# Products of the second MLP matrix on one pair of TensorE tiles, and its last chunk in four transfers

## The chip, the cores and the metric

The kernel runs on one core of a Trainium2 chip. The metric is the device time of one execution in microseconds (us); times are medians of several executions, all in the fast state where a state can be told. Profiles give the span on the core, about 1.3 us shorter than that time. In their lines PE is TensorE (PEld its weight loads), DVE is VectorE, ACT ScalarE, POOL GpSimd and SP SyncE, which issues the transfers.

## The reference, cut to what matters

A decode step for eight tokens mixes a windowed attention with an MLP, by a gate for each token:

```python
x = A_x                                                # 8 x 1 x 576
g = _sigmoid((x * gate_w).sum(-1, keepdims=True))
a = _A_ref(x, A_k_cache, A_v_cache, A_wq, A_wo)        # window of 2048, 16 kv heads of 128
b = _B_ref(x, B_w1, B_b1, B_w2, B_b2)                  # 576 -> 4608 -> 576
return g * a + (1 - g) * b
```

With so few tokens nearly all of the time goes into loading: 154 MB of cache and weights. `B_w2` (4608 x 576, 5.3 MB) comes last, in four chunks of 1152 rows, each as nine "rows" of 576 columns on 128 partitions.

## The kernel before

All output products, of the projection and of the second MLP matrix, add up in one accumulator bank. `hT` (128 x 8) is the stationary operand, and the kernel puts one product on a strip of 32 columns of the array. A row is two matmuls of 288 columns. With `split=2` odd rows go to a second pair of strips, so that four matmuls run together (in the trace four of chunk 0 start at 353.74 us, the next four 0.12 later):

```python
class AccGroup:
    def __init__(self, name, mms, deps, cost, after=(), prio=0, split=2):
        ...
            for i, (lhsT, rhs) in enumerate(grp.mms):
                for j in range(NJ):                        # NJ = 2
                    c = 64 * (i % split) + 32 * j          # which strip: 0, 32, 64, 96
                    ins = e.matmul(ps[c:c + 8, BK_ACC, 0:JN], lhsT, rhs[:, JN * j:JN * j + JN], start=False, stop=True,
                                   skip_group_check=True, tile_position=(0, c))
```

The chunks of the second matrix, and the end:

```python
def m2_chunk(ci):
    ...
    cuts = [0, 4, 8, 9] if ci == FC - 1 else [0, FJ]       # FC = 4 chunks, FJ = 9 rows
    ops = []
    for n, (j0, j1) in enumerate(zip(cuts, cuts[1:])):
        ...                                                # one transfer of rows j0 to j1
        mms = [(hT[:, FJ * ci + j, :], dst[:, j * D:(j + 1) * D]) for j in range(j0, j1)]
        ops.append(AccGroup("m2_%d_%d" % (ci, n), mms, [o_hT, d], cost=0.16 * (j1 - j0), after=o_m2[-1:], split=1 if ci == FC - 1 else 2).op)
        o_m2.append(ops[-1])
        if ci == FC - 1 and n == 0:                        # second pair of strips is complete: copy it out
            odd = [g_.op for g_ in acc_groups if g_.split == 2]
            o_ac.append(add("act", lambda e: e.activation(out=accs[0:40, :], in_=ps[64:104, BK_ACC, 0:JN], func=ACTF.Copy), deps=odd + pt_done[NG - 1], ...))
...
o_fin = add("dve", lambda e: e.tensor_tensor(out=out_sb[0:40, :], in0=ps[0:40, BK_ACC, 0:JN], in1=accs[0:40, :], op=ALU.add), deps=acc_ops + o_ac, ...)
# then two stores of 8 x 288
```

## Time and profile before

| | before |
|---|---|
| time | 366.93 us (366.67 to 367.24) |
| span of the profile | 365.7 us |
| DMA queue busy | 98.6% of the span |
| last landing to the end of the span | 3.03 us |
| granted TensorE clock in those 3 us | half (0.50) |

The first rows say that the transfers set nearly all of the time, the last two where a change of the products can act: behind the last landing. The prediction shows the lines and how they are read. "Landing" is here and below the 16th increment of a transfer's semaphore in the trace, the end of the span is taken as the last increment of the stores' semaphores, 0.02 us before the profile's own end, and a "gap" is the distance from the start of one group of concurrent matmuls to the next.

### The profile page before, as it was taken

To read this page: it belongs to the slowest core of one execution; us is meant where nothing else is said; L and a number is where in the kernel's file an instruction comes from. 1 tells how busy PE (TensorE), PEld (TensorE's weight loads), DVE (VectorE), ACT (ScalarE), POOL (GpSimd) and SP (SyncE) were. 2 spreads that over 40 slices of the span, in tenths; PEclk is the share of its full clock that TensorE was granted. 3 is DMA by queue.
4 is the path that set the end of the run, shared out by engine and by line. 5 is a ranking of instruction groups with operands and counts; after the bars stand their busy time and mean duration, and the time that the engine had idled before them with its cause. 6 is when DMAs were issued, how large, how long until landed. Compare 5 with 4: busy or idle time off the path is not lost.

```text
span 365.7 us, 3979 instructions
## 1 busy us (share of the span) xinstructions
PE 239.5 (65%) x1679; PEld 114.4 (31%) x1679; DVE 226.5 (62%) x340; ACT 22.3 (6%) x53; POOL 17.4 (5%) x80
## 2 busy tenths in 40 slices
PE   0269684838498948274959294838959397297666
PEld 0159331312143414121524132214414133143232
DVE  4700995675999280759974452689790739974321
ACT  1010000000000000000100000001000000010000
POOL 4021000001000000010000000000000000000000
PEclk9999998778599969596998678676978698878885
DMA  9999999999999999999999999999999999999994
GB/s 386 440 412 432 410 448 430 430 442 409 453 409 454 405 446 419 425 439 428 444 418 446 418 455 412 456 407 452 407 452 409 455 399 434 429 429 428 429 426 184
DMA packets 9546, 154.58 MB, mean 423 GB/s; under 512 B 1036, under 2 KB 1204, under 8 KB 2744
## 3 DMA queue, kind: packets, MB, share of 16 engines
q1 hardware_dynamic: 9472, 154.29, 98.6%
q8 instruction: 13, 0.21, 0.2%
q10 hardware_dynamic: 56, 0.03, 0.0%
q14 instruction: 5, 0.04, 0.0%
HBM read 154.31 MB, written 0.01 MB: 422 GB/s over the span
## 4 chain that ended last, share of the span: by engine, by line
DMA 63%; DVE 26%; PE 8%; issue 1%; SPq 0%; DVEq 0%
DMA arena<-in_A_k_cache_dram 54%; DVE arena L666 19%; DMA arena<-in_A_v_cache_dram 5%; PE ps L711 4%; PE ps L678 4%; DMA arena<-in_B_w_dram 4%; DVE arena L639 3%; DVE arena L597 1%; DVE arena L761 1%; DVE arena L631 1%; DVE arena L600 0%; PE ps L555 0%; DVE arena L606 0%; DVE arena L614 0%; PE ps L612 0%
## 5 line engine op out<-in xcount | busy, mean ns | idle before, releaser
L666 DVE STREAM_TRANSPOSE arena<-arena 128x4096 f32<-128x4096 f32 x32 | 140.7, 4424 | 84.8 <-DMA arena<-in_A_k_cache_dram 84.3
L678 PE MATMUL ps<-arena 128*32 128x512 bf16 x512 | 139.7, 435 | 63.0 <-DVE arena L666 63.0
L678 PEld LDWEIGHTS ps<-arena 128*32 128x32 bf16 x512 | 51.6, 104 | 143.7 <-DVE arena L666 68.0
L711 PE MATMUL ps<-arena 128*32 128x512 bf16 x512 | 62.1, 456 | 23.1 <-DVE arena L602 18.7
L711 PEld LDWEIGHTS ps<-arena 128*32 128x32 bf16 x512 | 25.3, 110 | 50.0 <-issue 32.1
L639 DVE STREAM_TRANSPOSE arena<-arena 128x512 bf16<-128x512 bf16 x32 | 30.8, 1020 | 0.0
L728 PE MATMUL ps<-arena 128*128 128x16 f32 x128 | 16.9, 264 | 5.6 <-ACT arena L722 3.9
L761 DVE COPY arena<-arena 32x4 bf16<-32x4 bf16 (+1 forms) x80 | 12.9, 161 | 11.7 <-POOL arena L749 9.6
L728 PEld LDWEIGHTS ps<-arena 128*128 128x128 f32 x128 | 15.5, 191 | 11.9 <-ACT arena L722 9.6
L722 ACT ACTIVATE arena<-ps 128x512 f32<-128x512 f32 x16 | 9.6, 597 | 149.8 <-PE ps L711 149.8
L749 POOL TENSOR_TENSOR arena<-arena 128x8 bf16<-128x8 f32 x30 | 5.8, 230 | 230.0 <-ACT arena L738 230.0
L555 PE MATMUL ps<-arena 128*8 128x288 bf16 (+1 forms) x140 | 10.5, 365 | 4.5 <-DMA arena<-in_B_w_dram 3.0
L510 PE MATMUL ps<-arena 128*128 128x8 bf16 x144 | 10.9, 201 | 2.6 <-DMA arena<-in_B_w_dram 2.6
L597 DVE TENSOR_REDUCE arena<-ps 128x1 f32<-128x512 f32 x8 | 5.5, 692 | 11.1 <-PE ps L678 11.0
L608 ACT ACTIVATE arena<-ps,arena 128x512 bf16<-128x512 f32 x8 | 5.5, 687 | 105.9 <-DVE arena L606 105.9
L510 PEld LDWEIGHTS ps<-arena 128*128 128x128 bf16 x144 | 10.8, 159 | 3.1 <-DMA arena<-in_B_w_dram 3.1
L659 POOL TENSOR_TENSOR arena<-arena 128x32 bf16<-128x32 bf16 x32 | 6.4, 239 | 86.1 <-PE ps L678 77.0
L612 PE MATMUL ps<-arena 128*128 128x32 f32 x16 | 3.7, 314 | 8.8 <-DVE arena L611 8.8
L631 DVE TENSOR_SCALAR arena<-arena 128x512 bf16<-128x512 bf16 x32 | 9.0, 324 | 0.0
L425 PE MATMUL ps<-arena 8*128 8x8 bf16 x8 | 0.6, 171 | 11.0 <-DVE arena L398 7.0
L555 PEld LDWEIGHTS ps<-arena 128*8 128x8 bf16 (+1 forms) x140 | 4.3, 98 | 9.8 <-DMA arena<-in_B_w_dram 5.0
L512 PE MATMUL ps<-arena 128*128 128x8 bf16 x36 | 7.2, 201 | 0.0
(84 smaller groups left out, 77.7 us busy)
## 6 DMA issues: line engine op xcount, KB each, us to landing
arena<-in_A_k_cache_dram SPq DMA_DIRECT2D x16, 4096.0 KB, 25.1
arena<-in_A_v_cache_dram SPq DMA_DIRECT2D x32, 2048.0 KB, 24.4
arena<-in_B_w_dram SPq DMA_DIRECT2D x1, 4608.0 KB, 23.9
arena<-in_A_wo_dram SPq DMA_DIRECT2D x4, 1152.0 KB, 10.0
arena<-in_A_wq_dram SPq DMA_DIRECT2D x1, 4096.0 KB, 13.4
arena<-in_B_w_dram SPq DMA_DIRECT2D x3, 1296.0 KB, 18.9
arena<-in_B_w_dram SPq DMA_DIRECT2D x3, 576.0 KB, 13.3
arena<-in_A_wq_dram SPq DMA_DIRECT2D x1, 512.0 KB, 3.6
```

What stands on the lines that cost most here:

```text
L510: ins = e.matmul(out_, lhsT, yT[:, kt, :], start=(kt == 0), stop=False)
L512: ins = e.matmul(out_, lhsT, yT[:, 4 + c // 2, :], start=False, stop=True)
L555: ins = e.matmul(ps[c:c + 8, BK_ACC, 0:JN], lhsT, rhs[:, JN * j:JN * j + JN], start=False, stop=True, skip_group_check=True, tile_position ...
L597: mx = add("dve", lambda e: e.tensor_reduce(out=k(MX), in_=ps[:, bank, :], axis=AXL.X, op=ALU.max), deps=[qk_done[g]], name="mx%d" % g, co ...
L631: return e.tensor_scalar(out=dst, in0=view("Pd").rearrange("p (s n) -> p s n", s=2), scalar1=amask[:, a:a + 1], scalar2=None, op0=ALU.mult)
L639: return e.transpose(dst, src)
L666: tr = add("dve", (lambda h=h, kb=kb: lambda e: e.transpose(bass.AP(arena_f, offset=foffs("KT") + kb * SE // 2, ap=[[AST // 2, 128], [4, 1 ...
L678: mm = e.matmul(ps[32 * c:32 * c + 32, 2 * (G % 2) + nb, :], qb[:, G % 2, n, 2 * h + ee, :], rhs, start=(h == 0 and t == 0), stop=(h == 1 ...
L711: mm = e.matmul(ps[c:c + 32, bk, :], PT[:, g % 2, 512 * q + 32 * t:512 * q + 32 * t + 32], slot(s)[:, 512 * t:512 * t + 512], start=(t < 2 ...
L722: u_ev[item] = add("act", lambda e: e.activation(out=EV[:, item % 2, :], in_=ps[:, bk, :].rearrange("p (r d j) -> p r j d", r=4, j=4), fun ...
L728: mm = e.matmul(ps[:, BK_S, OC + 16 * (item % 2):OC + 16 * (item % 2) + 16], EV[:, item % 2, 128 * r:128 * r + 128], i2[:, r, :, :].rearra ...
L761: return [add("dve", (lambda j=j, q=q: lambda e: e.tensor_copy(oT[32 * q:32 * q + 32, ch, j, bs], oN[32 * j:32 * j + 32, q, ch, bs]))(), d ...
```

## The change

Its evident intent: the products of all chunks go to the first pair of strips, so that the second pair is complete earlier and the copy out of it leaves the tail; and the last transfers become smaller, so that less is left to do when the last one lands.

```diff
-            cuts = [0, 4, 8, 9] if ci == FC - 1 else [0, FJ]
+            cuts = [0, 3, 6, 8, 9] if ci == FC - 1 else [0, FJ]
...
-                ops.append(AccGroup(..., split=1 if ci == FC - 1 else 2).op)
+                ops.append(AccGroup(..., split=1).op)
```

More of the change, by code (lines that the diff above doesn't have):

```diff
@@ L802, in m2_chunk @@
                 mms = [(hT[:, FJ * ci + j, :], dst[:, j * D:(j + 1) * D]) for j in range(j0, j1)]
-                ops.append(AccGroup("m2_%d_%d" % (ci, n), mms, [o_hT, d], cost=0.16 * (j1 - j0), after=o_m2[-1:], split=1 if ci == FC - 1 else 2).op)
+                ops.append(AccGroup("m2_%d_%d" % (ci, n), mms, [o_hT, d], cost=0.16 * (j1 - j0), after=o_m2[-1:], split=1).op)
                 o_m2.append(ops[-1])
```

## The prediction

> **What bounds the kernel now.** I read the page first: row 2, then the chain of waits (part 4), then the last 12 us as a timeline, the waits of those 12 us, and the busy time cut into the stretches of the TensorE clock.
>
> ```profile
> DMA  9999999999999999999999999999999999999994
> ...
> q1 hardware_dynamic: 9472, 154.29, 98.6%
> ...
> DMA 63%; DVE 26%; PE 8%; issue 1%; SPq 0%; DVEq 0%
> ```
>
> All but the last of the 40 slices have the DMA engines at 90% or more, and the one big queue fills 98.6% of the span. 154.3 MB have to come in, and the change alters no byte of that. So some 362 of the 366 us are out of its reach, and only what follows the last transfer can move. The end of the chain in order of time shows it:
>
> ```profile
> 348.63 0.33 SPq L798
> 349.00 13.30 DMA arena<-in_B_w_dram
> 362.35 1.38 PE ps L555 x10
> 363.76 0.45 DVE arena L826
> ```
>
> The last chunk of the second MLP matrix is issued at 348.6 and lands from 360.8 to 362.7; then come ten matmuls, one VectorE add (0.45), and the store, which ends the span at 365.7. The timeline of PE (start, length, engine, line, shape, count, idle time before and its releaser) is the part that the change works on:
>
> ```profile
> 353.74 0.78 PE L555 MATMUL ps<-arena 128*8 128x288 bf16 x18
> 356.35 2.32 PE L555 MATMUL ps<-arena 128*8 128x288 bf16 x34 [1.84 <-DMA arena<-in_B_w_dram]
> 359.45 2.50 PE L555 MATMUL ps<-arena 128*8 128x288 bf16 x26 [0.77 <-DMA arena<-in_B_w_dram]
> 362.35 1.36 PE L555 MATMUL ps<-arena 128*8 128x288 bf16 x10 [0.40 <-DMA arena<-in_B_w_dram]
> ```
>
> These are, in order: chunk 0 (18 matmuls: nine rows, two halves each), chunk 1 with the last output projection (18 + 16), chunk 2 with the first transfer of chunk 3 (18 + 8), and the other two transfers of chunk 3 (8 + 2). Chunk 0 took 0.78 us; chunk 2, the same work, took 1.35. The clock is why:
>
> ```profile
> 348.15:351.56 3.41, 2.35 (x34) 1.07 (x28) 0.00 (x0) 0.00 (x0) 0.00 (x0) 1.00 1.02 432
> 351.56:354.98 3.42, 2.49 (x36) 1.45 (x30) 0.97 (x7) 0.60 (x1) 0.00 (x0) 1.00 1.01 431
> 354.98:358.39 3.41, 2.04 (x34) 1.10 (x34) 1.85 (x12) 0.00 (x0) 0.00 (x0) 0.50 0.98 414
> 358.39:361.80 3.41, 2.63 (x32) 0.88 (x26) 0.00 (x0) 0.41 (x1) 0.00 (x0) 0.50 0.67 265
> 361.80:365.22 3.42, 1.51 (x12) 0.49 (x10) 0.45 (x1) 0.00 (x0) 0.00 (x0) 0.50 0.04 13
> ```
>
> The last three columns are clock, DMA share and GB/s. From 354.98 to the end PE has half its clock, just where it is on the path.
>
> [...]
> - [...] every stretch of one clock is a multiple of 3.41 us long, and there are two values only. [...]
> - [...] The matmul starts in the trace are 0.240 apart at half clock (361.02, 361.26, 361.50) and 0.122 at full (353.74, 353.86, 353.98).
> - [...] chunks 0 to 2 start four matmuls together, each on its own strip of 32 columns, then four more one gap later; chunk 3, already on the first pair, starts two per gap.
> - [...]
>
> **The change, part by part.** The instruction order of DVE, ACT, POOL and PE is unchanged; PE has one more wait, SP one more transfer.
>
> (a) *Pairs instead of fours in chunks 0 to 2.* 18 matmuls took five gaps (4, 4, 4, 4, 2); now they take nine. That is 4 gaps more per chunk: 0.49 us each at full clock, 0.96 at half. Chunks 0 and 1 have slack: PE idles 1.84 us before chunk 1 and 0.77 before chunk 2. Chunk 1 starts at 356.35; at half clock its nine gaps and the projection's four take it to 359.43, just in time for chunk 2 at 359.45. Only chunk 2's cost can reach the end.
>
> (b) *Three, three, two and one rows.* Packets of 1152 bytes start 0.047 us apart on one DMA engine, those of 4608 bytes 0.174. By interpolation, which is an estimate, 3456 bytes need 0.132 and 2304 need 0.089. With eight packets per engine the last chunk takes 8 x (2 x 0.132 + 0.089 + 0.047) = 3.20 us, was 8 x (2 x 0.174 + 0.047) = 3.16, plus one more completion. So the last landing goes from 362.65 to about 362.70. Counted back, the others land near 362.31 (eight rows; before also 362.31), 361.58 (six) and 360.5 (three). The semaphore counts in the trace gave 360.78, 362.31 and 362.65. Work after 362.31 shrinks from five pairs (four rows and one) to three.
>
> (c) *The clock.* This is the part that decides. I cut the whole trace into the 3.41 us windows and summed the time in which columns stream: columns over clock, matmuls started together counted once. Full-clock windows with a share of 0.375 or less (17 of them) were followed by half clock; those with 0.432 or more (41) by full clock, without exception. From half clock, it rose after shares of 0.687 and from 0.835 up, and stayed down after 0.633 and less, and once after 0.759. The window from 351.56 had 1.28 us of streaming (share 0.375) and lost the clock by a little. Its parts: the last value product 0.3, bias 0.12, [...] chunk 0 in five gaps 0.6. With nine gaps chunk 0 adds 0.48: 1.76 us, share 0.52. The clock stays full. Next window: chunk 1 nine gaps, projection four, 13 x 0.12 = 1.56 us, share 0.46, over 0.432, though narrowly. Next: chunk 2 (1.08) and five or six pairs of chunk 3 (some 0.65), share 0.5. So the tail runs at full clock.
>
> (d) *The ScalarE copy* (0.41 us) waited for chunk 2 and ended at 361.27; it now waits for the last projection. It had 2.5 us to spare, so it is worth nothing.
>
> **The sum at the end.** Before, eight rows' landing at 362.31, first pair 362.35, then 0.20, 0.24, 0.24 and 0.24: the ninth row's pair starts at 363.27, ends 0.44 later at 363.71, and the add starts at 363.76. After, at full clock: chunk 2 runs 359.45 to 360.55, three rows to 360.9, three more 361.62 to 362.0, two from 362.35 to 362.6. The last row waits for its landing at 362.70, starts at 362.74 and takes 0.286 (chunk 0's duration at full clock). So 363.03, and the add at 363.08. That is 0.68 us earlier; nothing behind it changes.
>
> **The rivals.**
> 1. *The clock stays at half.* Then PE is the bound: from 359.45 on chunks 2 and 3 are 18 pairs in a row, the last starting at 359.45 + 0.20 + 16 x 0.24 = 363.49 instead of 363.27, so 0.22 us slower (367.15). For it: the thin 0.46 against 0.432, a threshold read from one trace, and windows whose phase may differ between runs. Against it: I walked the tail through all phases of the window with those thresholds, and it ended at full clock in each; even if the clock drops once, the denser pairs fill a window by more than 0.69 and bring it back. I give this 15%.
> 2. *The tail of before was already at full clock in its timed runs.* In the same walk 6 of 35 phases give it that, ending 0.2 to 0.4 us earlier. Then the gain is 0.3 to 0.5 us. The three times spread over 0.57 us, so this can't be excluded.
> 3. *The transfers hide it all.* With a full clock the end follows the landing of the last row; smaller packets and a fourth completion push that back. For: the last row is already the release here. Against: they are issued 12 us before landing, behind a full queue, so issue costs nothing. By (b) it costs 0.05; even three times that leaves half a microsecond of gain.
> 4. *DMA or VectorE as the bound elsewhere*: unchanged, no part of the diff is there.
>
> **Range and chances.** 366.93 - 0.68 = 366.25 if the clock holds. Weighing 0.75 x (-0.68), 0.15 x (+0.22) and 0.10 x (-0.4) gives -0.52, so 366.4. I set 366.35. The runs of before spread by 0.3 us to each side of their median, and a median of a few runs may be off by 0.2; with rival 1 at the upper end the range is 365.8 to 367.0. Two per cent is 7.3 us, more than everything after the last landing (3 us), so faster or slower by that much would need something outside this tail: 0.01 each.
>
> **What would show it.** (a) chunk 0 as 18 matmuls over about 1.1 to 1.3 us instead of 0.78, starting in twos. (c) clock 1.00 in the stretches after 355 and starts 0.12 apart; at 0.50 with starts 0.24 apart and no idle time between chunk 2 and the end, rival 1 is right. (b) a PE wait on DMA ahead of the last pair, ending near 362.7 on the same scale; a landing past 362.9 means rival 3. (d) the ScalarE copy before 359.5. Sum: from the last matmul start to the end of the span 2.4 us as before less 0.16. The prediction is wrong if the clock falls back, or if the front of the kernel shifts by more than the tail can give, which would show at the first landing of chunk 0 (353.7).

What no run here shows is cut out of it and marked. The cuts take no term out of the sum at the end: it stays 366.93 - 0.68 = 366.25, and 366.35 with the rivals. They take one term out of the parts of the window from 351.56 in (c): there fp32 columns were given a weight that no run here tests. The recorded 1.28 us (share 0.375) and, with nine gaps, 1.76 us (0.52) still contain it. With every column counted alike, recounted from the same trace, they are 1.12 us (0.33) and 1.60 us (0.47), and the limits 0.375 and 0.432 become 0.33 and 0.42 for the same 17 and 41 windows, so the argument stands. What was cut about the ScalarE copy carried no number; in the trace the copy (360.86 to 361.27) and the pairs that PE starts at 360.82, 361.02 and 361.26 overlap.

## The result, and the profile after

366.26 us median of four runs (366.10 to 366.41), before 366.93. The ratio is 0.9981, 95% interval 0.9964 to 0.9999. Ratios here are the mean time of one kernel's fast runs over that of the other's of the same rounds, so not quite the ratio of the medians. As a difference it is 0.67 us.

The end of the chain of waits after (start, length, engine, line, count):

```profile
349.35 12.86 DMA arena<-in_B_w_dram
362.21 0.04 issue
362.26 0.67 PE ps L555 x6
362.95 0.45 DVE arena L826
```

Six matmuls in 0.67 us stand where ten in 1.38 us stood. The eight rows' landing is at 362.21, before it was at 362.31, so nearly the whole gain lies behind it. The timeline of PE after, to be laid beside the four lines in the prediction:

```profile
353.66 1.27 PE L555 MATMUL ps<-arena 128*8 128x288 bf16 x18
356.27 1.76 PE L555 MATMUL ps<-arena 128*8 128x288 bf16 x34 [1.35 <-DMA arena<-in_B_w_dram]
359.39 1.64 PE L555 MATMUL ps<-arena 128*8 128x288 bf16 x24 [1.35 <-DMA arena<-in_B_w_dram]
361.52 0.53 PE L555 MATMUL ps<-arena 128*8 128x288 bf16 x6 [0.49 <-DMA arena<-in_B_w_dram]
362.26 0.65 PE L555 MATMUL ps<-arena 128*8 128x288 bf16 x6 [0.20 <-DMA arena<-in_B_w_dram]
```

Chunk 0 takes longer (1.27 us for 0.78), in nine gaps of 0.12 us for five. But the second line, chunk 1 and the last projection, takes 1.76 us where fours took 2.32, and chunk 2 with three rows more (24 matmuls) 1.64. Less packing and yet faster: the clock column (third from the right) of the same stretches tells why. Before it stand the window, its length, and busy time and count of PE, PEld, DVE, ACT and POOL.

```profile
351.41:354.82 3.41, 2.94 (x36) 1.85 (x32) 0.90 (x6) 0.60 (x1) 0.00 (x0) 1.00 1.02 435
354.82:358.23 3.41, 1.87 (x36) 1.17 (x34) 1.92 (x12) 0.14 (x1) 0.00 (x0) 1.00 0.98 413
358.23:361.65 3.42, 1.77 (x28) 1.05 (x30) 0.00 (x0) 0.27 (x1) 0.00 (x0) 1.00 0.74 286
361.65:365.06 3.41, 1.06 (x12) 0.26 (x8) 0.45 (x1) 0.00 (x0) 0.00 (x0) 1.00 0.06 20
```

In this execution the clock stays full to the end, with streaming shares of 0.50, 0.47 and 0.47 in the first three windows. The share is taken as in the prediction, columns over clock and concurrent matmuls once, but with every column counted alike: 0.240 us for 288 at half clock, as the starts there lie apart, and half of that at full clock (the starts lie 0.122 apart).

### The profile page after: what moved, and what is told of

It reads as the page before. It is cut to its first block, busy times and chain, and to the rows that moved or that the text cites. A ratio compares the mean times of both kernels' runs of the same rounds, so it can differ in the third digit from the quotient of the medians.

```text
span 364.9 us, 3980 instructions
## 1 busy us (share of the span) xinstructions
PE 239.4 (66%) x1679; PEld 115.0 (32%) x1679; DVE 226.5 (62%) x340; ACT 22.4 (6%) x53; POOL 17.4 (5%) x80
## 3 DMA queue, kind: packets, MB, share of 16 engines
q1 hardware_dynamic: 9616, 154.29, 98.9%
## 4 chain that ended last, share of the span: by engine, by line
DMA 62%; DVE 24%; PE 11%; issue 1%; SPq 0%; DVEq 0%
DMA arena<-in_A_k_cache_dram 54%; DVE arena L666 18%; PE ps L678 6%; DMA arena<-in_A_v_cache_dram 5%; PE ps L711 4%; DMA arena<-in_B_w_dram 4%; DVE arena L639 3%; DVE arena L597 1%; DVE arena L631 1%; DVE arena L600 0%; DVE arena L606 0%; PE ps L612 0%; DVE arena L614 0%; PE ps L555 0%; SPq L798 0%
## 5 line engine op out<-in xcount | busy, mean ns | idle before, releaser
L555 PE MATMUL ps<-arena 128*8 128x288 bf16 (+1 forms) x140 | 9.3, 288 | 3.6 <-DMA arena<-in_B_w_dram 3.4
```

## The experiments

Theory: pairs stream longer than fours, and this keeps, or brings back, the full clock where PE is on the path; the finer transfers shorten the work behind the landing besides. Rivals: the transfers alone make the gain; or where the products go, with the earlier copy, makes it and the clock is a bystander. Ratios are to the kernel before in the same rounds; its nine runs beside the first four experiments had a median of 366.93, beside the next four 366.87.

The tails of all profiles, worked out from the semaphores and starts in the traces; half and full are granted clocks of 0.50 and 1.00. The moment of the last landing wanders from execution to execution, with either kernel, so the last column is the clean measure and the median time the noisy one:

| profile | clock at last landing | landing, us | to last matmul start | to end of span | median time (n) |
|---|---|---|---|---|---|
| before | half | 362.65 | 0.61 | 3.03 | 366.93 (4) |
| before, second | half | 362.32 | 0.61 | 3.02 | |
| before, third | half | 362.62 | 0.61 | 3.05 | |
| changed | full | 362.58 | 0.05 | 2.34 | 366.26 (4) |
| changed, again | full | 362.37 | 0.05 | 2.31 | 366.21 (5) |
| changed, third | full | 362.79 | 0.05 | 2.33 | |
| pairs only | full | 362.68 | 0.39 | 2.67 | 366.47 (5) |
| transfers only | full | 362.34 | 0.05 | 2.31 | 366.40 (5) |
| transfers only, second | half | 363.07 | 0.14 | 2.56 | |
| fours with idle matmuls | full | 362.39 | 0.19 | 2.47 | 366.34 (5) |
| pairs, thin chunks | full from 362.69 | 362.88 | 0.37 | 2.63 | 367.15 (5) |
| fours, thin chunks | half | 362.61 | 0.58 | 3.00 | 366.82 (5) |
| pairs, 5, 3, 1 rows | full | 362.43 | 0.05 | 2.31 | 366.17 (5) |
| all on one pair | full | 362.61 | 0.05 | 2.31 | 366.25 (5) |

### The changed kernel again

No edit.

> The changed kernel again, so that the other runs stand beside it on the same chip. All theories: 0.6 to 0.8 us faster than the kernel before; full clock (1.00) from about 351 us to the end of the span; last row's pair starts right after its landing.

Measured: 366.21 us, ratio 0.9979 (0.9966 to 0.9991). The gain repeats: 0.72 us. In this profile the clock was half until 353.11, two us longer than expected, and full from there to the end; the last pair started 0.05 us after its landing, as expected.

### Pairs only

```diff
-            cuts = [0, 3, 6, 8, 9] if ci == FC - 1 else [0, FJ]     # of the changed kernel
+            cuts = [0, 4, 8, 9] if ci == FC - 1 else [0, FJ]
```

> Products of chunks 0 to 2 on the first pair of tiles, but the last chunk in transfers of four, four and one rows as before. Clock theory (denser chunks 0 to 2 keep the TensorE clock at full): clock 1.00 after 355 us, after the landing of eight rows four pairs 0.12 apart and the last row's pair about 0.49 us after the first of them, so the end some 0.1 us later than the changed kernel and 0.5 to 0.6 us earlier than before. Rival (the finer transfers make the gain): no gain over before, within 0.15 us.

Measured: 366.47 us, ratio 0.9987 (0.9974 to 1.0000). So pairs alone give 0.46 us. The interval just reaches 1, but the tail of this profile is 0.36 us shorter than before's (2.67 against 3.03), and the fours with idle matmuls, below, gain without finer transfers too: the first rival, no gain without them, falls. But the expectation "full clock after 355" missed. In this profile the clock was half from 350.88 to 361.12, and the chain shows what that does to pairs:

```profile
353.80 1.89 PE ps L728 x8
355.69 7.69 PE ps L555 x80
363.40 0.45 DVE arena L826
```

PE ran without a pause from 355.7 on: the bound that the prediction gives as its first rival. After a window that such a stretch filled (share 1.0) the clock came back at 361.12, early enough to work off most of the backlog; the last pair was still 0.39 us late.

### Finer transfers only

```diff
-            cuts = [0, 4, 8, 9] if ci == FC - 1 else [0, FJ]        # of the kernel before
+            cuts = [0, 3, 6, 8, 9] if ci == FC - 1 else [0, FJ]
```

> Three, three, two and one rows, but chunks 0 to 2 on four tiles as before. My accounting: clock 0.50 from about 355 us as before; after the landing of eight rows pairs 0.20 and 0.24 apart, the last row's pair about 0.44 us after the first, and it takes 0.44 instead of 0.29 us, so some 0.25 us later than the changed kernel and 0.45 us earlier than before: the two parts overlap, each alone gives most of the gain. If the clock were all of it: no gain over before. If the finer transfers were all of it: as fast as the changed kernel.

> Finer transfers alone, one more profile; the first had full clock after 361.2 us by its windows' place. Clock theory: if the tail has half clock this time, pairs 0.20 and 0.24 apart after the landing of eight rows and 2.5 to 2.6 us from the last landing to the end of the span; at full clock 2.3 as in the first.

Measured: 366.40 us, ratio 0.9986 (0.9972 to 0.9999), 0.53 us less than before; expected was 0.45. The single run of the second profile took 366.93. The first profile (the fastest of its five runs, 365.94) had full clock from 361.21, against the expectation; the second had half to the end. Windows of the first, then the timeline of PE of the second:

```profile
357.80:361.21 3.41, 3.12 (x40) 1.22 (x40) 0.00 (x0) 0.41 (x1) 0.00 (x0) 0.50 0.75 292
361.21:364.62 3.41, 1.24 (x14) 0.36 (x12) 0.45 (x1) 0.00 (x0) 0.00 (x0) 1.00 0.08 28
```

```profile
356.82 2.33 PE L555 MATMUL ps<-arena 128*8 128x288 bf16 x34 [1.89 <-DMA arena<-in_B_w_dram]
359.95 3.71 PE L555 MATMUL ps<-arena 128*8 128x288 bf16 x36 [0.80 <-DMA arena<-in_B_w_dram]
```

In the second no gap shows between chunk 2 and the end, and the tail is 2.56 us, 0.47 less than before, as worked out ahead of it. In the first the tail is 2.31, the changed kernel's. So without pairs the clock is there in one execution and not in the other, by where the windows fall; the 0.53 us of the timed runs may hold both kinds, and 0.47 is what the smaller transfers give at half clock. The single run looks like no gain at all only because its last landing came at 363.07.

### Fours, with idle matmuls in between

```diff
+                    for lhsT, rhs in grp.mms[:grp.fill]:               # fill = 4 for chunks 0 to 2
+                        for j in range(NJ):
+                            ins = e.matmul(ps[32 * j:32 * j + 8, 0, 0:JN], lhsT, rhs[:, JN * j:JN * j + JN], start=True, stop=True,
+                                           skip_group_check=True, tile_position=(0, 32 * j))
```

One more edit is not shown: chunks 0 to 2 also wait for an exponential of the softmax. In the profile all of those are over by 323 us, 30 us before chunk 0, so this wait costs nothing.

> The kernel before (four tiles, transfers of four, four and one rows) with eight idle matmuls, in four pairs, repeated after each of chunks 0 to 2 into an unused accumulator bank: as much streaming time as the pairs have, without moving a product to other tiles and without an earlier ScalarE copy. Clock theory: full clock after 355 us and the same end as the kernel with pairs only, 0.5 to 0.6 us before the kernel before. Rival (where the products go, or the earlier copy, makes the gain): no gain, within 0.15 us.

Measured: 366.34 us, ratio 0.9983 (0.9970 to 0.9995), 0.59 us less than before. This kernel moves no product, keeps the old transfers, copies late, and computes 24 matmuls that nobody reads. It is faster all the same:

```profile
352.02:355.43 3.41, 2.32 (x38) 1.72 (x34) 1.53 (x10) 0.47 (x1) 0.00 (x0) 1.00 1.02 435
355.43:358.85 3.42, 2.69 (x40) 1.54 (x42) 1.29 (x9) 0.00 (x0) 0.00 (x0) 0.50 0.98 406
358.85:362.26 3.41, 2.46 (x44) 1.20 (x42) 0.00 (x0) 0.41 (x1) 0.00 (x0) 1.00 0.53 212
```

The clock was lost at 355.43 (share about 0.34 in the window before), and after the filled window that followed (0.79) it was back, at 358.85. So "full clock after 355" missed here too, but the clock was full at the last landing. The second rival, that the place of the products or the earlier copy makes the gain, falls.

### Thin chunks: pairs, and fours as a control

```diff
-                mms = [(...) for j in range(j0, j1)]
+                mms = [(...) for j in range(j0, j0 + 1 if ci < 2 else j1)]
```

Chunks 0 and 1 multiply one row of nine; the result is wrong (relative error 0.048 in both).

> The changed kernel with only one of nine rows multiplied in chunks 0 and 1 (a wrong result on purpose; loads, waits and order stay). That takes the streaming time out of the windows before chunk 2. Clock theory: half clock when chunk 2 starts, so its nine pairs and the nine of chunk 3 run one after the other 0.24 apart until a window full of them brings the clock back; last row's pair up to 0.8 us after its landing; 366.6 to 367.2 us, 0.4 to 0.9 slower than the changed kernel though it computes less. Rival (pairs, finer transfers or the earlier copy make the gain by themselves): as fast as the changed kernel, 366.2.

> The control: the kernel before with the same rows left out. Chunks 0 and 1 are off the path, so all theories: like before within 0.15 us (half clock in the tail, 3.0 us from the last landing to the end of the span). If it is much slower or faster than before, leaving the rows out does something else, and the run before it can't be read.

Measured: pairs 367.15 us, ratio 1.0004 (0.9991 to 1.0016); fours 366.82 us, ratio 0.9996 (0.9982 to 1.0009). The control is as before. The changed kernel, with 32 matmuls taken away from it, shows no gain any more in its timed runs. Windows and chain of the pairs, then the chain of the fours:

```profile
355.86:359.28 3.42, 1.53 (x18) 0.47 (x18) 1.31 (x9) 0.41 (x1) 0.00 (x0) 0.50 0.96 399
359.28:362.69 3.41, 2.96 (x26) 1.68 (x28) 0.00 (x0) 0.00 (x0) 0.00 (x0) 0.50 0.49 186
362.69:366.10 3.41, 0.84 (x14) 0.36 (x10) 0.45 (x1) 0.00 (x0) 0.00 (x0) 1.00 0.01 3
```

```profile
359.73 3.82 PE ps L555 x36
363.57 0.45 DVE arena L826
```

```profile
362.27 1.38 PE ps L555 x10
363.68 0.45 DVE arena L826
```

At half clock chunks 2 and 3 in pairs are 36 matmuls in one unbroken run, with PE the bound; the fours wait for their landing and then do ten. In this profile the clock returned at 362.69, for the last five pairs; the profiled run (366.89) was one of the faster. Its tail, 2.63 us, is still 0.4 shorter than before's, so the profile shows the backlog, and the loss of the gain rests on the five timed runs. That pairs without the clock are slower than fours is not resolved (spread of the five runs 1.0 us); a gain of more than 0.3 us is outside the interval.

### Five, three and one rows

```diff
-            cuts = [0, 3, 6, 8, 9] if ci == FC - 1 else [0, FJ]
+            cuts = [0, 5, 8, 9] if ci == FC - 1 else [0, FJ]
```

> The changed kernel with the last chunk in five, three and one rows: one transfer fewer, the same three pairs or rather four pairs after the landing of eight rows (three rows of the second transfer and the ninth). At full clock the three pairs take 0.37 us, as long as the ninth row takes to land, so my accounting: same as the changed kernel within 0.1 us. If the fourth transfer or the small last steps matter by themselves: 0.15 us or more slower.

Measured: 366.17 us, ratio 0.9981 (0.9968 to 0.9993): the changed kernel's time, with one transfer fewer. At full clock three rows (0.37 us) fit between the last two landings, 0.37 us apart, and the last pair starts 0.05 after its landing in both.

### All on one pair

```diff
-            def __init__(self, name, mms, deps, cost, after=(), prio=0, split=2):
+            def __init__(self, name, mms, deps, cost, after=(), prio=0, split=1):
...
-        e.tensor_tensor(out=out_sb[0:40, :], in0=ps[0:40, BK_ACC, 0:JN], in1=accs[0:40, :], op=ALU.add)
+        e.tensor_copy(out_sb[0:40, :], ps[0:40, BK_ACC, 0:JN])              # and no ScalarE copy
```

> The changed kernel with all output products, the projections too, on the first pair of tiles, so that nothing accumulates on the second: the ScalarE copy goes and the last VectorE add becomes a copy from the accumulator. More streaming time before the tail, so full clock at least as often. The last step 0.35 to 0.40 us instead of 0.45: 0.05 to 0.15 us faster than the changed kernel, from the shorter last step and a steadier clock. If the projections in pairs delay the last chunk: as fast or slower, with PE busy without idle time before the last landing.

Measured: 366.25 us, ratio 0.9983 (0.9971 to 0.9996): no faster than the changed kernel, an expectation missed (the changed kernel's runs stand in other rounds, on another chip; each has the kernel before beside it). The last step, a line of this kernel's VectorE timeline, is as long as the add's 0.45; the 0.35 to 0.40 us expected was a guess that rested on no run:

```profile
362.99 0.45 DVE L825 CAST arena<-ps 40x288 bf16<-40x288 f32 x1 [5.94 <-PE ps L555]
```

The second guess may hold: its five runs lie within 0.15 us, the narrowest of all, and its profile has full clock from 326.89 to 364.44. Five runs don't prove that.

### More profiles of both kernels

No edit.

> The kernel before, one more profile: does its tail have half clock in another execution too, where the 3.41 us windows lie otherwise? Clock theory: half clock at the last landing in most executions, and then 3.0 to 3.1 us from the last landing to the end of the span; with full clock there 2.4 to 2.5 us.

> The same again: half clock at the last landing and 3.0 to 3.1 us from there to the end, or full clock and 2.4 to 2.5 us; nothing between unless the clock changes after the landing.

> The changed kernel, a third profile. Clock theory: full clock at the last landing again and 2.3 us from there to the end of the span.

Measured, one run each: 366.64 and 366.98 us before, 366.41 changed. The table has the tails: before three times half and 3.02 to 3.05 us, changed three times full and 2.31 to 2.34. But the way there differed. Windows and one line of the PE timeline of the third profile of the changed kernel:

```profile
350.69:354.11 3.42, 3.07 (x19) 1.19 (x14) 0.00 (x0) 0.60 (x1) 0.00 (x0) 0.50 1.01 431
354.11:357.52 3.41, 3.41 (x26) 2.41 (x28) 1.79 (x12) 0.00 (x0) 0.00 (x0) 0.50 0.99 419
357.52:360.93 3.41, 3.41 (x40) 1.90 (x38) 1.03 (x7) 0.12 (x1) 0.00 (x0) 0.50 0.80 313
360.93:364.35 3.42, 2.19 (x36) 1.33 (x30) 0.45 (x1) 0.28 (x1) 0.00 (x0) 1.00 0.11 42
```

```profile
355.30 7.82 PE L555 MATMUL ps<-arena 128*8 128x288 bf16 x88
```

Here the clock was half for three windows, PE had a backlog of all 88 matmuls, and after the full window up to 360.93 the clock was back just in time: the last pair again started 0.05 us after its landing. The clock had been lost after the window from 347.28 (share 0.37), before the first matmul that the change touches. Pairs hold the clock in one execution and win it back in another.

No version beat the changed kernel; the one with five, three and one rows equals it with a transfer fewer.

## Why the prediction was right

Its sum, 366.93 - 0.68 = 366.25 if the clock holds, met 366.26; the number, 366.35, carried 0.1 us for the rivals. The sum is confirmed where it was made, in the tail (0.69 us shorter, worked out 0.68). That the medians agree to 0.01 us is luck: the four runs before alone spread by 0.57 us.

- *What bounds it.* Right. The queue is as full after (98.9%), and the tail alone shrank, from 3.03 to 2.34 us.
- *(a) Pairs.* Chunk 0 took 1.27 us, within the 1.1 to 1.3 given, and chunks 0 and 1 were off the path in the first profile after. In the third they were not: all 88 matmuls ran on end, their slack gone.
- *(b) Transfers.* Landings were forecast near 360.5, 361.58 and 362.31, and came at 360.40, 361.48 and 362.21. The 0.05 us by which the last one should have slipped can't be seen: last landings lie between 362.32 and 362.65 before and between 362.37 and 362.79 after. That the smaller transfers shorten the work behind the landing is shown alone: 2.56 us at half clock, where before had 3.03.
- *(c) The clock.* Right in its outcome: full at the last landing in all three profiles. Its sign, full clock in the stretches after 355, came in two of them; in the third the clock was half until 360.93, which the prediction had named as a way to be wrong. The streaming shares in the first, 0.50, 0.47 and 0.47, were forecast as 0.47 (0.52 with the term that is cut), 0.46 and 0.5. The two thresholds, read off one trace "without exception", are blurred in fourteen: as far as these record the clock (from some 44 us on), a window up to 0.36 always lost the full clock and one above 0.38 always kept it (between, both happened); half clock rose after every share of 0.78 or more, and never below 0.68. Busy time does not stand in for the share: before, the clock was lost at 354.98 after a window in which the profile counts PE busy for 2.49 of 3.42 us, and the longest idle time that touches that window lasted 1.84 us. The firm part is the fallback that the prediction gave in half a sentence, that a dropped clock is brought back by the denser pairs; the third profile shows just that (PE busy for 3.41 of 3.41 us up to 360.93, then full clock).
- *(d) The copy.* It ran at 358.09, 2.8 us earlier, and is worth nothing: fours with idle matmuls copy late (360.62) and gain all the same, and in the third profile of the changed kernel it ran at 360.81, as late as before (360.86), with the full gain in the tail.
- *Rival 1* did not come in the result, but is real: the thin chunks produce it. *Rival 2*, before at full clock, was seen in none of three profiles, which doesn't exclude it for its fastest runs. *Rival 3* falls: a transfer more or less makes no difference (366.17 and 366.21 us).

Two gains that overlap add up badly, and the prediction did not say how much each part gives. Alone, the transfers give 0.53 us and the pairs 0.46; together they give 0.7. The finer transfers leave less to do behind the landing, which is worth less when each step is twice as fast (starts 0.12 us apart for 0.24).

Still open: how the clock is decided when the share lies between the limits under (c), and how much slower than fours pairs are without the clock.

## What to carry to other kernels

Before packing matmuls onto more tiles, ask whether PE is the bound there. Here it waited for transfers anyway, so packing only made it idler (chunk 0 took 0.78 us for 1.27), and the clock that it lost was missing in the tail (3.03 us for 2.34). Read the clock in the windows before the tail, not in the mean. And measure such a tail from the last landing, as the landing itself wanders by more than the effect.
